# Clustered attention into an MLP on one core: a new order for the opening list, and a hand-over from attention to MLP in written order up to MLP step 14

## The chip, the cores and the metric

One core of a Trainium2 chip runs the whole program in one launch. The time is device microseconds of one execution; the figure given for a kernel is the median of several runs. The engines are TensorE (PE), VectorE (DVE), ScalarE (ACT), GpSimd (POOL) and SyncE (SP, which here only issues DMAs).

## The reference

Attention over 2 batches, 8 heads, 768 positions and 64 features, in which a query sees only the keys of its own cluster (argmax of the products with 16 normed centroids), followed by two MLP layers of 512 to 2048 to 512 on all 1536 tokens.

```python
q_assign = np.argmax(np.einsum('bhsd,hcd->bhsc', q_n, c_n), axis=-1)
k_assign = np.argmax(np.einsum('bhsd,hcd->bhsc', k_n, c_n), axis=-1)
mask = q_assign[:, :, :, None] == k_assign[:, :, None, :]
scores = np.where(mask, scale * np.matmul(q, k.transpose(0, 1, 3, 2)), -1000000000.0)
attn = np.exp(scores - np.max(scores, axis=-1, keepdims=True))
x = np.matmul(attn / (np.sum(attn, axis=-1, keepdims=True) + 1e-09), v)
...
h = x @ w_in
g = np.maximum(h, 0.0) + alpha * np.minimum(h, 0.0)
x = g @ w_out
...
h = x @ w_in2
return (np.maximum(h, 0.0) + np.log1p(np.exp(-np.abs(h)))) @ w_out2
```

## The kernel before

Matrix products run on PE in pairs of a high and a low part of each operand (a cast to fp32r, and what the cast left out), so that one product of the reference is two or three matmuls.

**Attention.** The work is cut into 8 pairs (batch, two heads) of 12 units each, so 96 units; a unit is 128 queries of one head against all 768 keys, and one unit is begun at every tick. A unit goes through `scores` (PE, L599 the products and L600 the cluster rows that serve as the mask), `maxima` (DVE, nm L605), `exps` (ACT, e L614), `transposes` (PE, pt L627), `highs` (ACT, ph L643), `lows` (DVE, pl L647), `attend` (PE, o L657) and `drain` (the copy tmp on ACT, L680 or L684, and the sum into xs on DVE or POOL, L682 or L691). While a pair is being worked on, the next pair's operands are made: `high_k`, `high_q` (ACT, hi L369, L372), `low_q` (DVE, lo L388), squares, folds and their norms (`inv_norm`, L131 to L140: ACT, then DVE or POOL), products with the centroids (dps L403), their copy (dsb L411), transposes (dt L428), normed products and one-hot rows (dn, mx, oh, L442 to L476), the mask rows (mq, mk, L507, L511). The tables STEADY, FIRST, SECOND, THIRD and LAST give for each of these steps the tick of the pair at which it is issued. The list PRELUDE is the order of the steps ahead of unit 0 and of those of pair 1 that stand with them ("hiq0 1" is `high_q` of the first half for pair 1; "warm 14" is 14 idle transposes on PE, wps L212). The order of instructions on the engines is the order in which the program issues them, by `man`, a manual schedule of all five engines, until `man.close()` at L814, which is tick 96 (NU): from there on a scheduler of the compiler orders the instructions.

**The end of a pair.** `finish` (L698) divides a pair's sums by its softmax sums and splits the result into xh and xl, the MLP's input: reciprocals (rs L721), their spread (rx, ACT L729), transposes (rp, PE L739), multiplication (xs, DVE L745), high (xh, ACT L752) and low part (xl, POOL L757). FINISH and FINISH_LAST give the ticks, counted from the pair's end.

**The MLP.** Two layers of 16 slices of 128 hidden features, in 3 groups of 512 tokens: 96 steps. Step k has a `first` product (hp, 12 matmuls, L876), an activation (`activate`: n and hp on ACT, L888, L889; `complete`: hp on DVE L909, gh on ACT L916, gl on DVE L917) and a `second` product (acc, 12 matmuls, L935); 96 x 24 = 2304 matmuls. BLOCKS groups the slices into runs whose sums stay in PSUM; `close` adds a run's sums to y (copy L947, additions L950). The weights come as float64 words and are converted on the chip: two halves of a slice (w_in, w_out), each one load and stages of m (ACT L164), r (ACT L167), L168, L171, L173 on DVE, t (POOL L178), high (ACT ih or oh, L180) and low (POOL il or ol, L181). There are five buffers for slices. Slices 0 and 1 are converted during the last attention ticks, their steps spread over the ticks; slices 2 to 6 in one go each, at these points:

```python
for F, k in ((2, -1), (3, 0), (4, 1)):
    due[k].append(F)
for F in range(5, 2 * NF):
    due.setdefault(last_use[F - 5], []).append(F)
```

The functions that the change touches stand here with the line numbers of the profile.

Of the kernel before, what the change touches and what calls it, by code (L numbers as in the profile page):

```python
# [9 lines left out]
F32 = mybir.dt.float32  # L10
# [23 lines left out]
    dl0=12, dl1=12, inv0=12, de0=12.5, de1=12.5, inv1=12.5, inv2=13, dt=13, dn=13.5, op0a=13.5, mx=14,  # L34
# [16 lines left out]
FINISH_LAST = [1, 2, 2, 3, 6, 7, 8, 9, 9]  # L51

BLOCKS = ((2, 4, 4, 4, 2), (4, 4, 4, 4))
P = 128
# [4 lines left out]
def kernel(  # L59
# [124 lines left out]
    def convert(F, pool, temp):  # L184
        layer, f = divmod(F, NF)
        w_in, w_out = (w_in1, w_out1) if layer == 0 else (w_in2, w_out2)
        tiles = [pool.tile([P, DM], F32R, tag=tag, name=tag) for tag in ("ih", "il", "oh", "ol")]
        weights[layer, f] = tiles
        return (
            to_float32(tiles[0], tiles[1], w_in[f].rearrange("p c n -> p (c n)"), temp),  # L190
            to_float32(tiles[2], tiles[3], w_out[f], temp),
        )


    with ExitStack() as actx:
# [110 lines left out]
        def steps_of(n):  # L306
# [56 lines left out]
            def high_k(t):  # L363
                if t == 0:
# [333 lines left out]
        def finish(n):  # L698
# [6 lines left out]
            ks = FINISH_LAST if last else FINISH  # L705
# [26 lines left out]

            for t in range(2):

                @at_(u0 + ks[4 + t])
                def _(t=t):
                    rp_ = ps_m.tile([P, 512], F32, tag="m", name="rp_")
# [6 lines left out]
                    xs = xs_[n]  # L744
                    nc.vector.tensor_tensor(out=xs[:, halves[t]], in0=xs[:, halves[t]], in1=rp_[:, 0:HS], op=ALU.mult)  # L745
# [36 lines left out]
        at(1)(lambda: warm(8))  # L782
# [29 lines left out]
        while u < NU + LAG + 2 or todo:  # L812
            if u == NU:
                man.close()  # L814
# [24 lines left out]
        man.close()  # L839

    gp = ctx.enter_context(tc.tile_pool(name="gp", bufs=2, reuse_waits="tile"))
    sp = ctx.enter_context(tc.tile_pool(name="sp", bufs=1, reuse_waits="tile"))
    cp = ctx.enter_context(tc.tile_pool(name="cp", bufs=2, side="right", reuse_waits="tile"))
    ps_h = ctx.enter_context(tc.tile_pool(name="ps_h", bufs=4, space=PSUM, reuse_waits="tile"))
    ps_a = ctx.enter_context(tc.tile_pool(name="ps_a", bufs=1, space=PSUM, reuse_waits="tile"))

    steps, starts, ends = [], set(), set()  # L850
    for layer in range(2):
        f0 = 0
        for size in BLOCKS[layer]:
            starts.add((layer, f0))
            ends.add((layer, f0 + size - 1))
            steps += [(layer, g, f) for g in range(NG) for f in range(f0, f0 + size)]
            f0 += size
    NS = len(steps)
    hps = {}
    mids = {}  # L860
    acts = {}
    accs = {}
    sums_ = {}

    def first(k):
        if k >= NS:
            return
        layer, g, f = steps[k]
        ts = slice(g * G, (g + 1) * G)
        h_, l_ = weights[layer, f][0:2]  # L870
        hp = ps_h.tile([P, G], F32, tag="h", name="hp")
        n = 0
        for c in range(NC_):
            cs = slice(c * P, (c + 1) * P)
            for a_, b_ in ((h_, xh), (h_, xl), (l_, xh)):
                nc.tensor.matmul(hp, lhsT=a_[:, cs], rhs=b_[:, c, ts], start=n == 0, stop=n == 3 * NC_ - 1)  # L876
                n += 1
        hps[k] = hp
# [194 lines left out]
```

## Time and profile before

| | |
|---|---|
| median of 3 runs | 807.25 us (805.39 to 807.45) |
| the profiled execution | 806.27 us |
| its span, first to last instruction | 804.5 us |
| mean granted TensorE clock | 0.987 |
| PE busy | 780.4 us, 97% |
| DVE busy | 585.3 us, 73% |
| ACT busy | 496.0 us, 62% |
| POOL busy | 356.8 us, 44% |

The span lies 1.8 us under the execution's own time. The profile's times are microseconds from the span's start. PE's matmuls overlap: a row's duration is longer than the distance to the next row, and it is the distance that counts. Of the span, attention takes roughly the first 270 us, the MLP the rest.

### The profile page before, as it was taken

What the parts mean: (1) busy time and instruction counts of PE and PEld (TensorE: products, weight loads), DVE (VectorE), ACT (ScalarE), POOL (GpSimd) and SP (SyncE); (2) the same over time, 40 slices, a digit from 0 to 9 for tenths busy, and PEclk for the clock granted to TensorE, in tenths of its full rate; (3) what the DMA queues carried; (4) which work ended last, traced back from release to release, by engine and by line L of the source; (5) the groups of instructions that cost most, each with busy time, mean ns of one, the idle gap of its engine ahead of it and who ended that gap; (6) DMA issues with size and microseconds to landing.
All of it is one profiled execution on the core that took longest, in us unless ns stands there. A gap on an engine that the chain in (4) does not pass through costs nothing.

```text
span 804.5 us, 11964 instructions
## 1 busy us (share of the span) xinstructions
PE 780.4 (97%) x4139; PEld 666.7 (83%) x4139; DVE 585.3 (73%) x923; ACT 496.0 (62%) x1024; POOL 356.8 (44%) x380
## 2 busy tenths in 40 slices
PE   6899999999998979999999999999999999999998
PEld 6789999999997758888888888888888888888886
DVE  7689989989989977547646835978469569765444
ACT  5788999999999778346536535674366245343221
POOL 6567668778354775026115404585144036023000
PEclk9899999999999989999999999999999999999999
DMA  9666667655552343102302401312014012000002
GB/s 265 180 166 172 152 170 173 182 145 128 119 144 64 105 157 132 53 26 79 105 0 72 138 1 53 132 53 78 1 53 156 2 53 81 24 2 1 28 31 97
DMA packets 26955, 75.91 MB, mean 94 GB/s; under 512 B 4464, under 2 KB 7408, under 8 KB 26896
## 3 DMA queue, kind: packets, MB, share of 16 engines
q1 hardware_dynamic: 26896, 75.16, 32.3%
q8 instruction: 32, 0.52, 0.3%
q14 instruction: 27, 0.22, 0.1%
HBM read 49.36 MB, written 3.15 MB: 65 GB/s over the span
## 4 chain that ended last, share of the span: by engine, by line
PE 78%; DVE 11%; ACT 3%; POOL 3%; issue 3%; DMA 1%; SPq 0%; DVEq 0%; POOLq 0%; ACTq 0%
PE acc L935 29%; PE hp L876 27%; PE pt L627 6%; PE o L657 6%; PE s L599 3%; PE s L600 3%; DVE r L173 2%; DVE pl L647 2%; POOL t L178 1%; DVE nm L605 1%; PE dps L403 1%; DVE m L168 1%; DVE y L950 1%; DVE lo L388 1%; ACT e L614 1%
## 5 line engine op out<-in xcount | busy, mean ns | idle before, releaser
L876 PE MATMUL hp<-xh,ih 128*128 128x512 f32 x384 | 150.2, 392 | 1.3 <-ACT e L614 1.3
L876 PE MATMUL hp<-xl,ih 128*128 128x512 f32 x384 | 150.1, 391 | 0.0
L876 PE MATMUL hp<-xh,il 128*128 128x512 f32 x384 | 149.9, 391 | 0.0
L181 POOL TENSOR_TENSOR il<-t,ih 128x512 fp32r<-128x512 f32 x32 | 44.3, 1385 | 198.7 <-ACT ih L180 188.3
L917 DVE TENSOR_TENSOR gl<-hp,gh 128x512 fp32r<-128x512 f32 x96 | 65.9, 686 | 69.6 <-ACT gh L916 69.5
L916 ACT CAST gh<-hp 128x512 fp32r<-128x512 f32 x96 | 56.4, 587 | 88.8 <-PE acc L935 69.9
L605 DVE TENSOR_REDUCE nm<-s 128x1 f32<-128x768 f32 x96 | 90.9, 947 | 18.3 <-PE s L600 18.3
L647 DVE TENSOR_TENSOR pl<-pt,ph 128x384 fp32r<-128x384 f32 x192 | 97.3, 548 | 5.8 <-ACT ph L643 4.9
L178 POOL TENSOR_TENSOR t<-m,r 128x512 uint32<-128x512 uint32 x64 | 85.6, 1337 | 30.8 <-DVE r L173 16.3
L643 ACT CAST ph<-pt 128x384 fp32r<-128x384 f32 x192 | 84.0, 485 | 14.7 <-PE pt L627 14.1
L614 ACT ACTIVATE e<-s,nm 128x768 f32<-128x768 f32 x96 | 87.9, 916 | 3.0 <-DVE nm L605 2.4
L898 ACT ACTIVATE sp<-a 128x512 f32<-128x512 f32 x48 | 30.4, 632 | 92.5 <-DVE a L894 92.5
L627 PE MATMUL pt<-ident,e 128*128 128x128 f32 x576 | 83.2, 277 | 4.1 <-DVE pl L647 4.0
L876 PEld LDWEIGHTS hp<-xh,ih 128*128 128x128 f32 x384 | 72.4, 189 | 16.5 <-ACT e L614 1.6
L876 PEld LDWEIGHTS hp<-xh,il 128*128 128x128 f32 x384 | 72.5, 189 | 15.2
L876 PEld LDWEIGHTS hp<-xl,ih 128*128 128x128 f32 x384 | 72.4, 189 | 15.1
L627 PEld LDWEIGHTS pt<-ident,e 128*128 128x128 f32 x576 | 66.9, 141 | 16.4 <-DVE pl L647 13.0
L935 PE MATMUL acc<-gh,oh 128*128 128x512 f32 x192 | 72.6, 395 | 5.4 <-ACT gh L916 5.4
L935 PE MATMUL acc<-gl,oh 128*128 128x512 f32 x192 | 75.7, 394 | 0.2 <-DVE gl L917 0.2
L935 PE MATMUL acc<-gh,ol 128*128 128x512 f32 x192 | 75.2, 392 | 0.0
L935 PE MATMUL acc<-ol,gh 128*128 128x512 f32 x192 | 74.7, 389 | 0.0
L935 PE MATMUL acc<-oh,gh 128*128 128x512 f32 x192 | 74.7, 389 | 0.0
(171 smaller groups left out, 1671.8 us busy)
## 6 DMA issues: line engine op xcount, KB each, us to landing
raw<-in_w_in_dram SPq DMA_DIRECT2D x32, 512.0 KB, 3.3
raw<-in_w_out_dram SPq DMA_DIRECT2D x32, 512.0 KB, 3.3
tok<-in_qk_tok_dram SPq DMA_DIRECT2D x8, 768.0 KB, 6.1
ak<-hi SPq DMA_DIRECT2D x31, 192.0 KB, 3.0
dim<-in_qk_dim_dram SPq DMA_DIRECT2D x6, 768.0 KB, 5.4
aq<-hi SPq DMA_DIRECT2D x16, 192.0 KB, 3.6
aq<-lo SPq DMA_DIRECT2D x16, 192.0 KB, 4.1
rawv<-in_v_dram SPq DMA_DIRECT2D x8, 384.0 KB, 3.5
```

What stands on the lines that cost most here:

```text
L178: nc.gpsimd.tensor_tensor(out=t.bitcast(U32), in0=mu, in1=r, op=ALU.add)
L181: nc.gpsimd.tensor_tensor(out=low, in0=t, in1=high.bitcast(F32), op=ALU.subtract)
L605: nc.vector.tensor_reduce(out=nm, in_=st[u]["s"][:, :, 0:HS], axis=AX.XY, op=ALU.max, negate=True)
L614: nc.scalar.activation(out=e.rearrange("p (a j) c -> p a (j c)", a=2), in_=st[u]["s"][:, :, 0:HS], func=AF.Exp, bias=st[u]["nm"], scale=1. ...
L627: nc.tensor.transpose(pt[:, j * P : (j + 1) * P], st[u]["e"][:, 3 * a + j, :], ident)
L643: nc.scalar.copy(out=dh, in_=src)
L647: nc.vector.tensor_tensor(out=dl, in0=src, in1=dh.bitcast(F32), op=ALU.subtract)
L657: nc.tensor.matmul(acc[key][:, 0:QG], lhsT=vv[:, j, 2 * hh : 2 * hh + 2, :].rearrange("p a d -> p (a d)"), rhs=grp[key][part][:, j, :], st ...
L876: nc.tensor.matmul(hp, lhsT=a_[:, cs], rhs=b_[:, c, ts], start=n == 0, stop=n == 3 * NC_ - 1)
L916: nc.scalar.copy(out=gh, in_=hp)
L917: nc.vector.tensor_tensor(out=gl, in0=hp, in1=gh.bitcast(F32), op=ALU.subtract)
L935: nc.tensor.matmul(accs[c], lhsT=a_, rhs=b_, start=opens and n == 0, stop=closes and n == 2)
```

## The change

It has two parts.

**The opening.** In PRELUDE the steps of pair 1 that cast its operands (hiq, hik), the centroid operands of pair 0 (op0a to op0c) and `values` stand ahead of pair 0's norm (inv0), and pair 1's low parts (lq0, lq1) stand around the norm and no longer behind the one-hot rows. Pair 2's inv2 comes half a tick later. The eight warm transposes at tick 1 are gone.

**The hand-over.** Pair 6 is finished at earlier ticks (FINISH_NEXT), pair 7 at nearer and in halves (FINISH_LAST; `multiply` and `rest_of_x` of their own). The conversions of slices 0 and 1 begin one tick earlier, the w_in halves first; slices 2 and 3 are no longer begun during the units. `head` puts slice 0's first product for token group 0 on PE at tick NU - 3 = 93, with its activation at 94 and 95, and that for group 1 (step 1 in the new blocks) at tick 99. The manual order goes on to MLP step 14; in it the tables BESIDE and LOADS say at which step a half of a slice is converted and loaded, and its last stage is issued a step later (`last_stages`). From step 14 on the scheduler orders as before. The first block of layer 0 has two slices and so has the second. The five weight buffers lie in two pools, of 2 and 3.

The diff, cut to what moves work:

```diff
 SECOND = dict(
-    dl0=12, dl1=12, inv0=12, de0=12.5, de1=12.5, inv1=12.5, inv2=13, dt=13, dn=13.5, op0a=13.5, mx=14,
+    dl0=12, dl1=12, inv0=12, de0=12.5, de1=12.5, inv1=12.5, dt=13, inv2=13.5, dn=13.5, op0a=13.5, mx=14,
...
 PRELUDE = [
...
-    "lq1 0", "sq0 0", "dk0 0", "dq0 0", "red0 0", "sq1 0", "dk1 0", "dq1 0", "red1 0", "inv0 0", "de0 0",
...
+    "lq1 0", "sq0 0", "dk0 0", "dq0 0", "red0 0", "sq1 0", "dk1 0", "dq1 0", "red1 0", "op0a 0", "op0b 0",
...
-FINISH_LAST = [1, 2, 2, 3, 6, 7, 8, 9, 9]
-
-BLOCKS = ((2, 4, 4, 4, 2), (4, 4, 4, 4))
+FINISH_LAST = [0.5, 1, 1, 1, 2, 4, 2, 4, 2]
+
+FINISH_NEXT = [3, 4, 5, 5, 6, 7, 7, 8, 9]
+
+BLOCKS = ((2, 2, 4, 4, 4), (4, 4, 4, 4))
+
+SLOTS = 5
+
+BESIDE = {2: (2, 1), 3: (3, 1), 4: (4, 0), 5: (4, 1), 6: (5, 0), 7: (6, 0), 8: (5, 1), 9: (6, 1), 12: (7, 0), 13: (7, 1)}
+
+LOADS = {3: 4, 5: 5, 6: 6, 11: 7}
...
-            ks = FINISH_LAST if last else FINISH
+            ks = FINISH_LAST if last else FINISH_NEXT if n == len(pairs) - 2 else FINISH
...
+            if last:
+                at_(u0 + ks[6])(lambda: rest_of_x(halves[0]))
+                at_(u0 + ks[7])(lambda: rest_of_x(halves[1]))
+            else:
+                at_(u0 + ks[8])(lambda: rest_of_x(slice(0, S)))
...
-        at(1)(lambda: warm(8))
...
-        for F in range(4):
-            todo[NU - 14 if F < 2 else NU - 12 + 6 * F, L].append(lambda F=F: begin(F))
-            for j in range(2):
-                start = NU - 12 + 3 * (2 * F + j)
-                for n, wait in enumerate((0, 2, 3, 4, 5, 6, 8) if F < 2 else (0,)):
-                    tick = NU - 14 if n == 0 and 2 * F + j < 3 else start + wait
-                    todo[tick, L].append(lambda F=F, j=j: next(started[F][j]))
+        for F in range(2):
+            todo[NU - 14, L].append(lambda F=F: begin(F))
+        for m, (j, F) in enumerate((j, F) for j in range(2) for F in range(2)):
+            for n, wait in enumerate((0, 2, 3, 4, 5, 6, 9)):
+                tick = NU - 14 if n == 0 and m < 3 else NU - 13 + 3 * m + wait
+                todo[tick, L].append(lambda F=F, j=j: next(started[F][j]))
+
+
+        def head(k):
+            if k == 0:
+                first(k, ps_m.tile([P, 512], F32, tag="m", name="hp"))
+            else:
+                both = ps_s.tile([P, 2, 512], F32, tag="s", name="hp")
+                first(k, both[:, 0])
+
+        todo[NU - 3, L].append(lambda: head(0))
+        todo[NU - 2, L].append(lambda: activate(0))
+        todo[NU - 1, L].append(lambda: complete(0))
+        todo[NU + 3, L].append(lambda: head(1))
+        todo[NU + 4, L].append(lambda: activate(1))
+        todo[NU + 5, L].append(lambda: complete(1))
...
-            if u == NU:
-                man.close()
...
-    for F, k in ((2, -1), (3, 0), (4, 1)):
-        due[k].append(F)
-    for F in range(5, 2 * NF):
-        due.setdefault(last_use[F - 5], []).append(F)
+    for F in range(8, 2 * NF):
+        due[max(14, last_use[F - SLOTS])].append(F)
...
+    def beside(F, j):
+        for _ in range(5):
+            next(fresh[F][j])
+        ready.append(fresh[F][j])
+
+    def last_stages():
+        while ready:
+            next(ready.pop())
...
+    for k in range(2, NS):
+        if k == 14:
+            man.close()
+        if k in LOADS:
+            load(LOADS[k])
...
         complete(k + 1)
-        if k < 2:
+        last_stages()
+        if k in BESIDE:
+            beside(*BESIDE[k])
+        if k >= 14:
             conversions(k)
         first(k + 2)
         activate(k + 2)
         second(k)
         close(k)
-        if k >= 2:
-            conversions(k)
```

How the instructions stand in a row, before and after, at three places (the changed kernel's line numbers differ from those of before). ACT in the opening, from pair 0's squares (sq) to pair 1's; before:

```order
L329 ACTIVATE sq<-tok 128x768 x2
L131 ACTIVATE s_236<-ss,tiny 128x24
L132 ACTIVATE s_236<-s_236 128x24
L411 COPY dsb<-dps 64x384 x2
L542 CAST mq<-hi 64x768
L369 CAST hi<-dim 128x384 x2
L372 ACTIVATE hi<-dim 128x384 x2
L329 ACTIVATE sq<-tok 128x768 x2
```

and now:

```order
L411 ACTIVATE sq<-tok 128x768 x2
L628 CAST mq<-hi 64x768
L458 ACTIVATE hi<-dim 128x384 x2
L454 CAST hi<-dim 128x384 x2
L138 ACTIVATE s_254<-ss,tiny 128x24
L139 ACTIVATE s_254<-s_254 128x24
L497 COPY dsb<-dps 64x384 x2
L411 ACTIVATE sq<-tok 128x768 x2
```

The mq copy and pair 1's casts (L369, L372; now L454, L458) have moved from behind the norm (s_236, s_254) and the copy of the centroid products (dsb) to ahead of both.

DVE in the opening, around pair 0's one-hot rows (oh), from the normed products to unit 0's maxima (nm); before:

```order
L442 TENSOR_TENSOR dn<-dt,rinv 128x384
L454 TENSOR_REDUCE mx<-dn 128x24
L462 TENSOR_TENSOR dn<-dn,mx 128x384
L463 TENSOR_TENSOR dn<-dn,rank 128x384
L473 TENSOR_REDUCE m_326<-dn 128x24
L476 TENSOR_TENSOR oh<-dn,m_326 128x384
L388 SCALAR_TENSOR_TENSOR lo<-dim,hi 128x384 x2
L511 TENSOR_SCALAR mk<-ot,mscale,mbias_96 16x384 x2
L605 TENSOR_REDUCE nm<-s 128x1 x2
```

and now:

```order
L474 SCALAR_TENSOR_TENSOR lo<-dim,hi 128x384
L528 TENSOR_TENSOR dn<-dt,rinv 128x384
L540 TENSOR_REDUCE mx<-dn 128x24
L548 TENSOR_TENSOR dn<-dn,mx 128x384
L549 TENSOR_TENSOR dn<-dn,rank 128x384
L559 TENSOR_REDUCE m_328<-dn 128x24
L562 TENSOR_TENSOR oh<-dn,m_328 128x384
L597 TENSOR_SCALAR mk<-ot,mscale,mbias_96 16x384 x2
L691 TENSOR_REDUCE nm<-s 128x1 x2
```

The two low parts of pair 1 no longer stand between the one-hot rows and the mask rows (mk); one of them stands ahead of the normed products, the other further up.

PE at the end of the units, from unit 95's scores (the last) to slice 0's first MLP product (hp); before:

```order
L599 MATMUL s<-ak,aq 128x384
L600 MATMUL s<-mk,mq 128x384
L627 MATMUL pt<-ident,e 128x128 x6
L657 MATMUL o<-pl,vv 128x256 x6
L739 MATMUL rp__4314<-ident,rx 128x128 x3
L627 MATMUL pt<-ident,e 128x128 x6
L876 MATMUL hp<-xh,ih 128x512
L876 MATMUL hp<-xl,ih 128x512
L876 MATMUL hp<-xh,il 128x512
```

and now, from the last units' transposes (pt) and attend matmuls (o) to the second product, that for token group 1:

```order
L743 MATMUL o<-ph,vv 128x256 x6
L713 MATMUL pt<-ident,e 128x128 x6
L743 MATMUL o<-pl,vv 128x256 x6
L743 MATMUL o<-ph,vv 128x256 x6
L831 MATMUL rp__4323<-ident,rx 128x128 x3
L743 MATMUL o<-pl,vv 128x256 x6
L831 MATMUL rp__4340<-ident,rx 128x128 x3
L232 MATMUL hp<-xh,ih 128x512
L232 MATMUL hp<-xl,ih 128x512
L232 MATMUL hp<-xh,il 128x512
```

The last attention work (o) and pair 7's reciprocals (rp) stand now ahead of that product; before, part of it stood behind the first hp product. The product for group 0 stands between the attend matmuls of one tick and the scores of unit 93:

```order
L713 MATMUL pt<-ident,e 128x128 x6
L743 MATMUL o<-pl,vv 128x256 x6
L232 MATMUL hp<-xh,ih 128x512
L232 MATMUL hp<-xl,ih 128x512
L232 MATMUL hp<-xh,il 128x512
```

## Rows read from the trace of the kernel before

**Rows 1.** The waits of PE: line waited for, us in total, times, longest.

```profile
PE acc L935 <- ACT gh L916: 5.4, 1, 5.4
```

**Rows 2.** Busy time by stretch (x instructions), then PE's granted clock, DMA share, GB/s.

```profile
22.00:32.00 10.00, 9.03 (x45) 7.68 (x43) 5.64 (x10) 5.91 (x16) 3.51 (x7) 0.67 0.74 215
...
80.00:240.00 160.00, 159.99 (x1201) 149.30 (x1200) 145.60 (x258) 149.82 (x365) 107.67 (x141) 1.00 0.61 153
...
250.00:260.00 10.00, 8.04 (x55) 6.69 (x56) 9.72 (x18) 9.06 (x22) 3.49 (x4) 1.00 0.35 114
```

**Rows 3.** Timeline of DVE, opening: start us, us, engine, line, operation.

```profile
14.49 0.57 DVE L463 TENSOR_TENSOR dn<-dn,rank 128x384 f32<-128x384 f32 x1
...
16.16 3.32 DVE L388 SCALAR_TENSOR_TENSOR lo<-dim,hi 128x384 fp32r<-128x384 f32 x2
...
19.51 1.26 DVE L511 TENSOR_SCALAR mk<-ot,mscale,mbias 16x384 fp32r<-16x384 f32 x2
```

**Rows 4.** Timeline of ACT, opening.

```profile
10.70 0.31 ACT L131 ACTIVATE s<-ss,tiny 128x24 f32<-128x24 f32 x1 [1.36 <-DVE ss L340]
...
11.90 0.84 ACT L542 CAST mq<-hi 64x768 fp32r<-64x768 f32 x1
...
13.46 0.94 ACT L372 ACTIVATE hi<-dim 128x384 fp32r<-128x384 f32 x2
```

**Rows 5.** Timeline of POOL, opening.

```profile
13.69 1.82 POOL L383 TENSOR_TENSOR lo<-dim,hi 128x768 fp32r<-128x768 f32 x1 [4.06 <-ACT hi L369]
...
15.95 5.09 POOL L348 TENSOR_TENSOR sq<-sq 128x768 f32<-128x768 f32 x6 [0.43 <-ACT sq L329]
```

**Rows 6.** Timeline of PE, opening.

```profile
16.70 0.53 PE L492 MATMUL ot<-identr,oh 128*64 128x128 f32 x6
...
20.92 0.41 PE L600 MATMUL s<-mk,mq 80*128 80x384 f32 x1 [3.47 <-DVE mk L511]
...
25.32 1.97 PE L212 MATMUL wps<-ident 128*128 128x128 f32 x8
```

**Rows 7.** Timeline of PE, hand-over and the program's last matmul.

```profile
263.92 0.61 PE L876 MATMUL hp<-xh,ih 128*128 128x512 f32 x1 [1.34 <-ACT e L614]
...
297.21 2.08 PE L935 MATMUL acc<-gh,oh 128*128 128x512 f32 x4 [5.38 <-ACT gh L916]
...
800.41 0.39 PE L935 MATMUL acc<-oh,gl 128*128 128x512 f32 x1
```

**Rows 8.** The chain that ended last, in order of time, about 305 us.

```profile
305.29 2.72 PE acc L935 x12
```

**Rows 9.** Timeline of DVE around the hand-over.

```profile
247.60 1.75 DVE L168 TENSOR_SCALAR m<-m 128x512 f32<-128x512 f32 x1
...
265.39 1.02 DVE L647 TENSOR_TENSOR pl<-pt,ph 128x384 fp32r<-128x384 f32 x2
...
266.42 1.49 DVE L173 SCALAR_TENSOR_TENSOR r<-raw,r 128x512 uint32<-128x512 uint32 x1
...
273.46 0.54 DVE L745 TENSOR_TENSOR xs<-xs,rp__4331 128x384 f32<-128x384 f32 x1
...
274.98 1.40 DVE L171 TENSOR_SCALAR m<-m 128x512 uint32<-128x512 uint32 x1
```

**Rows 10.** Timeline of ACT after the last unit's low parts.

```profile
269.98 0.36 ACT L680 COPY tmp<-o 64x256 f32<-64x256 f32 x1 [0.33 <-PE o L657]
```

**Rows 11.** Groups by line, all of the program: busy us, mean ns, idle before.

```profile
L173 DVE SCALAR_TENSOR_TENSOR r<-raw,r 128x512 uint32<-128x512 uint32 x64 | 61.8, 965 | 2.0 <-ACT r L167 1.0 <-issue 0.4
...
L950 DVE TENSOR_TENSOR y<-y,acc 128x512 f32<-128x512 f32 x84 | 54.9, 680 | 10.0 <-PE acc L935 10.0
...
L171 DVE TENSOR_SCALAR m<-m 128x512 uint32<-128x512 uint32 x64 | 48.8, 762 | 1.1
...
L168 DVE TENSOR_SCALAR m<-m 128x512 f32<-128x512 f32 x64 | 45.0, 704 | 12.4 <-ACT m L164 12.2
...
L909 DVE SCALAR_TENSOR_TENSOR hp<-n,nalpha,hp 128x512 f32<-128x512 f32 x48 | 35.9, 749 | 34.1 <-ACT hp L889 34.1
```

More of the change, by code (lines that the diff above doesn't have):

```diff
@@ L192, in convert, with first @@
         )
+    stage = {}
+    msteps, starts, ends = [], set(), set()
+    for layer in range(2):
+        f0 = 0
+        for size in BLOCKS[layer]:
+            starts.add((layer, f0))
+            ends.add((layer, f0 + size - 1))
+            msteps += [(layer, g, f) for g in range(NG) for f in range(f0, f0 + size)]
+            f0 += size
+    NS = len(msteps)
+    hps = {}
+    mids = {}
+    acts = {}
+    accs = {}
+    sums_ = {}
+    def first(k, hp=None):
+        if k >= NS:
+            return
+        layer, g, f = msteps[k]
+        ts = slice(g * G, (g + 1) * G)
+        h_, l_ = weights[layer, f][0:2]
+        if hp is None:
+            hp = stage["ps_h"].tile([P, G], F32, tag="h", name="hp")
+        n = 0
+        for c in range(NC_):
+            cs = slice(c * P, (c + 1) * P)
+            for a_, b_ in ((h_, xh), (h_, xl), (l_, xh)):
+                nc.tensor.matmul(hp, lhsT=a_[:, cs], rhs=b_[:, c, ts], start=n == 0, stop=n == 3 * NC_ - 1)
+                n += 1
+        hps[k] = hp
@@ L743, in _ @@
                         )
-                    xs = xs_[n]
-                    nc.vector.tensor_tensor(out=xs[:, halves[t]], in0=xs[:, halves[t]], in1=rp_[:, 0:HS], op=ALU.mult)
+                    if not last:
+                        multiply(t)
+                if last:
+                    at_(u0 + ks[4 + t])(lambda t=t: multiply(t))
             where = slice(b * S, (b + 1) * S)
@@ L848 @@
     ps_a = ctx.enter_context(tc.tile_pool(name="ps_a", bufs=1, space=PSUM, reuse_waits="tile"))
[L850 to L878, printed above, removed]
@@ L961, with slice_, load @@
     last_use = {}
-    for k, (layer, g, f) in enumerate(steps):
+    for k, (layer, g, f) in enumerate(msteps):
         last_use[layer * NF + f] = k
     due = defaultdict(list)
-    for F, k in ((2, -1), (3, 0), (4, 1)):
-        due[k].append(F)
-    for F in range(5, 2 * NF):
-        due.setdefault(last_use[F - 5], []).append(F)
+    for F in range(8, 2 * NF):
+        due[max(14, last_use[F - SLOTS])].append(F)
     def temp(which, dtype):
         return cp.tile([P, DM], dtype, tag=which, name=which, bufs=4 if which == "raw" else 2)
+    def slice_(F):
+        return convert(F, stage["wpool"] if F % SLOTS < 2 else wpool2, temp)
     def conversions(k):
         for F in due.get(k, []):
-            for gen in started.pop(F, None) or convert(F, stage["wpool"], temp):
+            for gen in slice_(F):
                 for _ in gen:
                     pass
-    conversions(-2)
-    first(0)
-    activate(0)
-    conversions(-1)
-    first(1)
-    complete(0)
-    activate(1)
-    for k in range(NS):
+    fresh = {}
+    ready = []
+    def load(F):
+        fresh[F] = slice_(F)
+        for gen in fresh[F]:
+            next(gen)
+    def beside(F, j):
[5 more added lines that the diff above has]
+            next(ready.pop())
+    load(2)
+    load(3)
+    second(0)
+    beside(2, 0)
+    first(2)
+    activate(2)
+    second(1)
+    close(1)
+    last_stages()
+    beside(3, 0)
+    first(3)
+    complete(2)
+    activate(3)
+    for k in range(2, NS):
[3 more added lines that the diff above has]
+            load(LOADS[k])
         if k == NS - 3:
```

108 lines of the change are left out of this document (58 added, 50 removed), and 9 rows, old and new, of the table PRELUDE.

## The prediction

> **What bounds the kernel now.** I read the windows first, then the waits of PE, then the timelines of two stretches: the opening (9 to 30 us) and the hand-over from the last attention units to the MLP (250 to 305 us). In the windows the reader sees that PE never stands from 80 to 240 us: 159.99 of 160 us busy at full clock [rows 2]. So time saved ahead of that stretch shifts all that follows, and time saved inside it on another engine is worth nothing. Two stretches differ: 22 to 32 us, where PE is busy 9.03 of 10 but at a granted clock of 0.67, and 250 to 260 us, where PE works 8.04 of 10 and DVE 9.72. The waits show one long stall behind that, 5.4 us on ACT's high part [rows 1], and the timelines show the rest: 3.47 us in the opening on DVE's mask rows [rows 6], 1.34 us ahead of the first MLP product [rows 7]. The program ends when PE does: its last matmul starts at 800.41 us [rows 7]; with the pitch of 2.72/12 = 0.23 [rows 8] PE ends at 800.64.
>
> **The opening.** (a) ACT: the copy to mq and four casts of pair 1 move ahead of the norm's first ACT step. They ran from 11.90 to 14.40, 2.50 us; ACT had stood 1.36 us before 10.70 [rows 4]. The norm starts 2.50 - 1.36 = 1.14 us later. (b) DVE: one low part of pair 1 now goes between rinv and dn. A two-input DVE operation of that shape took 0.57 [rows 3]; beside POOL the two low parts took 3.32, or 1.66 each [rows 3]. I take 0.57, since POOL has no fold to do that early; the other one goes into the time in which DVE now waits for the later norm. (c) The masks no longer stand behind these two. Their transposes were done at 16.70 + 0.53 = 17.23 [rows 6], the masks began at 19.51 [rows 3]: 2.28 us go. Unit 0's scores come 2.28 - 1.14 - 0.57 = 0.57 us earlier. (d) The eight warm matmuls ahead of unit 2's scores, 1.97 us of PE [rows 6], go; what lies next there are the products for unit 2, whose inputs were loaded early. Together 2.54; I take **2.5 us**. Bounds: with 1.66 in (b) and nothing from (d), because unit 2 then waits for its operands' DMAs, -0.5; with (b) hidden wholly, 3.1. The later first step of pair 2 (inv2 moved) costs nothing while POOL and DVE have gaps there; if they had none it would stay inside these bounds.
>
> A rule of the Trainium skill speaks against (b) and (c). The rows first: DVE's two-input subtraction at 14.49 took 0.57 while POOL's own subtraction ran from 13.69 to 15.51 [rows 3, 5], so it was not held up; the low parts, which began at 16.16 while POOL folded from 15.95 to 21.04, were [rows 3, 5]. SBUF — State Buffer, section "SBUF: two separate sides", in the Trainium skill says that DVE and GpSimd share a pair of ports by an exclusive lock, and that a DVE operation with two SBUF inputs blocks for the whole of the other's instruction. The first row disagrees, the second agrees. Without the rule the opening gives 2.5; with it, about nothing (rival C).
>
> **The hand-over.** Let T be the end of the last unit's low parts on DVE: before, 265.39 + 1.02 = 266.41 [rows 9]. From there to PE's end it took 800.64 - 266.41 = 534.23 us. What changes:
> (e) T moves back. Slice 0's first product (12 matmuls, 2.72 us by a chain row of 12 [rows 8]) now stands on PE ahead of unit 93's scores, and its activation puts two operations on DVE ahead of T: 0.75 for hp [rows 11] and about as much for the subtraction, 1.5. At most both count: 4.2. At least nothing: PE had 1.96 us free between 250 and 260 us [rows 2], and conversions that DVE does there could slide. DVE is at 9.72 of 10 [rows 2], so its 1.5 counts fully; the product comes ahead of PE's free time and delays the maxima on which DVE waits, so most of it counts. I take **3.6**, nearer the upper end: T = 270.0.
> (f) After T a short chain remains until slice 0's second product: the copy to tmp, the sum into xs, the transposed reciprocals, two multiplications. Before, tmp's start to the end of the multiplication was 269.98 to 274.00 [rows 9, 10], 4.0 us with other work between; without that work I take 3.7 (2.0 to 4.0).
> (g) From there PE has 2304 - 12 matmuls at 2.72/12 us [rows 8]: 519.5 us.
> (h) The clock: PE stands in (f), and after a stand it worked slowly. After 5.38 us, four matmuls took 2.08 us where 0.91 is their full-clock time; the first hp after 1.34 us took 0.61 [rows 7]. I take 2.0 in all: 1.2 from four, and a few more; ends 0 and 3.4 (twelve of them at that pace).
> (i) A new wait. Slice 7's first half is begun at step 12 and its last stage is at step 13, where product 15 reads it: no whole step of slack. DVE's part of a half conversion is 0.70 + 0.76 + 0.97 = 2.43 us at the means [rows 11], 1.75 + 1.40 + 1.49 = 4.64 when each is held up by POOL [rows 9]. A stall of 0 to 2.2; I take 1.0. The other conversions have a step or more. The late ACT high part that cost 5.38 us [rows 7] goes because slices 2 to 6 are now spread over steps instead of standing ahead of it in ACT's queue.
> Sum behind T: 3.7 + 519.5 + 2.0 + 1.0 = 526.2 against 534.23: 8.0 less, of which 3.6 is given back by T: **4.4 us** gained.
>
> In all 2.5 + 4.4 = 6.9 us off the profiled execution's 806.27 us, whose median of runs is 807.25 (0.98 more; I keep to the profiled one, which lies within the runs shown): 799.4, and I say **799.5**. A measurement of this kernel can tell 0.3%, 2.4 us, from no change: "same" is 804.8 to 809.7.
>
> **Rivals.**
> B, the units' end does not move and PE stays fast: the product fits into PE's free 1.96 us and DVE's slack, no low clock, no stall in (i). 799.5 - 3.6 - 2.0 - 1.0 = 792.9. For it: PE's free time before T; against: DVE at 9.72 of 10 [rows 2].
> C, the opening gives nothing: DVE's chain to the masks is held up by POOL's folds, which now begin earlier because the squares on ACT do. Two hold-ups of 1.3 to 1.8 us (a POOL operation is 1.82 [rows 5]) eat the 2.5. 802.0. For it the low parts' 1.66; against it the 0.57 [rows 3].
> D, no change: all at the far end, T back by 4.2, opening -0.5, (h) 2.6, (i) 2.2: 799.5 + 0.6 + 3.0 + 0.6 + 1.2 = 804.9.
> E, slower: the written order becomes the bound in steps 2 to 13. Engines do there what is written and can't fill a wait with later work. A step is 24 matmuls, 5.44 us. DVE needs 1.5 of it for the activation and, in three of these twelve steps, four additions of 0.68 [rows 11], 0.68 per step in the mean; that leaves 3.3 for a half conversion. At the held-up 4.64 [rows 9] each of twelve steps would be 1.3 longer: 16 us, 815. It decides from a mean of 4.15, where the loss of 0.85 x 12 = 10.2 lifts 799.5 over 809.7. Against it: the means sum to 2.43 over all 64 [rows 11].
> That the change doesn't do what it says I set aside: the order of instructions shows the moves.
>
> **How the numbers follow.** Forecast 0.50 (796.5 to 803 by its own bounds), B 0.14, C 0.17, D 0.11, E 0.08. The forecast, B and C are faster by over 0.3%, less 0.02 for their upper fringe: 0.79. Same: D and that fringe, 0.13. Slower: E, 0.08. The range runs from B's 793 to a little past D, 806; left out are E, half of B's lower side and D's upper side, under 0.2.
>
> **What would show it.** In the changed profile: no wait of PE on the mask rows near 3.5 us but one near 2.9, unit 2's scores about 2.5 us earlier; PE standing not over 1 us at a time from 245 us to T; T near 267.5, which is 270.0 less the opening's 2.5; slice 0's second product some 3.7 behind T at a low clock for a few matmuls; no 5.4 us on the high part; a wait of about 1 us at product 15. The forecast is wrong if T moves by more than 4.2 against the opening's shift (D), if PE waits in steps 2 to 13 again and again (E), or if unit 2's scores come no earlier (C).

## The result: slower, by the wait of one temporary, a late block and an opening that gives its gain back

| kernel | median us | runs | ratio to before, 95% interval |
|---|---|---|---|
| before, same chip | 806.28 | 805.39 to 807.45 | 1 |
| changed | 817.47 | 812.31 to 819.02 | 1.0117 (1.0098 to 1.0136) |
| changed, a second time beside another before (806.91) | 812.78 | 808.82 to 814.07 | 1.0070 (1.0047 to 1.0092) |

The forecast of 799.5 us, range 793 to 806, was wrong in its sign. The first measurement's three longer executions (817 to 819 us) have a mean granted TensorE clock of 0.981, the two shorter ones 0.986 and 0.987. The profiled execution of the changed kernel took 813.88 us, 7.6 more than before's 806.27, and its last matmul starts at 807.85 us for 800.41 [rows 7]. I use it for all that follows; PE's end is 0.23 later, as in the forecast.

The waits of PE in the changed kernel (line waited for, us in total, times, longest):

```profile
PE o L743 <- DVE xs L768: 6.3, 2, 4.5
PE dt L514 <- ACT dsb L497: 6.3, 2, 4.9
PE pt L713 <- DVE pl L733: 4.9, 6, 1.6
PE acc L973 <- DVE gl L273: 4.5, 3, 2.8
...
PE hp L232 <- ACT ih L187: 1.2, 1, 1.2
PE dps L489 <- DMA aq<-lo: 1.1, 1, 1.1
```

The 5.4 us on the high part gh [rows 1] are gone. What has come: 4.5 us of an attend matmul on xs, 4.9 in the opening (on the same copy of the centroid products, dsb, before waited 2.1 at the longest), 2.8 of a second product on the low part, and the 1.2 of product 15 that the forecast had named. The windows show the stretch of the units' end in the changed kernel (columns as in [rows 2]: PE, PEld, DVE, ACT, POOL, granted clock):

```profile
250.00:260.00 10.00, 9.56 (x67) 8.21 (x67) 8.99 (x15) 7.18 (x18) 5.08 (x5) 1.00 0.22 67
260.00:270.00 10.00, 7.39 (x45) 5.61 (x43) 6.96 (x13) 7.86 (x18) 4.16 (x4) 1.00 0.00 1
270.00:280.00 10.00, 5.01 (x24) 4.71 (x25) 4.74 (x11) 5.49 (x12) 1.22 (x3) 0.66 0.00 0
```

and, behind the 8.04 us of PE from 250 to 260 us [rows 2], in before:

```profile
260.00:270.00 10.00, 8.38 (x44) 6.98 (x44) 9.87 (x16) 8.66 (x20) 7.85 (x6) 0.83 0.23 81
270.00:280.00 10.00, 10.00 (x57) 8.60 (x56) 8.81 (x14) 7.18 (x14) 5.75 (x5) 1.00 0.39 131
```

In the changed kernel no engine is full from 260 to 280 us: all wait for one another. The granted clock averages 0.66 from 270 us on, part of the stretch at each of its two levels (0.5 is 1.2 GHz, 1 is 2.4 GHz). The cause stands in ACT's and POOL's timelines. ACT:

```profile
256.28 0.64 ACT L187 CAST ih<-t 128x512 fp32r<-128x512 f32 x1
259.74 0.66 ACT L174 ACTIVATE r<-raw 128x512 uint32<-128x512 uint32 x1 [2.82 <-POOL t L185]
260.31 0.89 ACT L700 ACTIVATE e<-s,nm 128x768 f32<-128x768 f32 x1
...
267.25 0.67 ACT L187 CAST ih<-t 128x512 fp32r<-128x512 f32 x1
270.78 0.66 ACT L174 ACTIVATE r<-raw 128x512 uint32<-128x512 uint32 x1 [2.86 <-POOL t L185]
271.34 0.57 ACT L272 CAST gh<-hp 128x512 fp32r<-128x512 f32 x1
271.93 0.36 ACT L766 COPY tmp<-o 64x256 f32<-64x256 f32 x1
272.32 0.90 ACT L700 ACTIVATE e<-s,nm 128x768 f32<-128x768 f32 x1
```

and POOL:

```profile
257.00 1.28 POOL L188 TENSOR_TENSOR il<-t,ih 128x512 fp32r<-128x512 f32 x1 [4.49 <-ACT ih L187]
258.23 1.47 POOL L185 TENSOR_TENSOR t<-m,r 128x512 uint32<-128x512 uint32 x1
...
268.06 1.47 POOL L188 TENSOR_TENSOR il<-t,ih 128x512 fp32r<-128x512 f32 x1 [5.84 <-ACT ih L187]
269.49 1.26 POOL L185 TENSOR_TENSOR t<-m,r 128x512 uint32<-128x512 uint32 x1
```

The temporary r of a conversion has one buffer. The change issues a half conversion's last stage (ih, il) one tick later against its other stages, wait 9 for 8. In that tick POOL now has il of one half ahead of t of the next, and ACT has r of the half after that directly behind ih. So ACT's r waits for t, t stands behind il, and il waits for ih on ACT: 0.6 + 1.3 + 1.5 us in a row, twice, while behind ACT's r the exps of the last units and the copy to tmp wait. PE's timeline shows what follows from it, and the waits behind (in the first row the attend matmul that wants xs, which wants tmp; the third row is slice 0's first product for token group 1, the fourth product 15, and the last one stands at the end of layer 0):

```profile
273.14 1.65 PE L743 MATMUL o<-ph,vv 128*128 128x256 f32 x6 [4.47 <-DVE xs L768]
...
279.20 0.98 PE L743 MATMUL o<-ph,vv 128*128 128x256 f32 x6 [1.85 <-DVE xs L768]
...
281.46 0.48 PE L232 MATMUL hp<-xh,ih 128*128 128x512 f32 x1
...
356.95 0.50 PE L232 MATMUL hp<-xh,ih 128*128 128x512 f32 x1 [1.19 <-ACT ih L187]
...
376.02 0.50 PE L973 MATMUL acc<-gl,oh 128*128 128x512 f32 x1 [1.55 <-DVE gl L273]
...
562.46 0.96 PE L973 MATMUL acc<-oh,gl 128*128 128x512 f32 x3 [2.77 <-DVE gl L273]
```

The difference in three pieces, cut at unit 80's scores and at the end of the last unit's low parts, which in the changed kernel are this row of DVE:

```profile
275.98 1.20 DVE L733 TENSOR_TENSOR pl<-pt,ph 128x384 fp32r<-128x384 f32 x2 [0.91 <-ACT ph L729]
```

Unit 80's scores start at 224.57 us (before 221.43): 3.1 us lost in the opening and the units behind it. From there to the end of unit 95's low parts it took 52.6 us; the forecast had 270.0 - 221.43 = 48.6. From these low parts to PE's end it took 530.9 us; the forecast had 526.2. So against the forecast 5.6 us are missing in the opening (it had 2.5 gained), 4.0 at the units' end and 4.7 behind, 14.4 in all (rounded). Against before, cut at the same two places, the last two pieces took 52.6 us for 51.5 and 530.9 for 527.7: the change lost 3.1, 1.1 and 3.2 us there.

### The profile page after: what moved, and what is told of

The parts are those of the page before. It is cut to its first block, busy times and chain, and to the rows that moved or that the text cites. A ratio compares the mean times of both kernels' runs of the same rounds, so it can differ in the third digit from the quotient of the medians.

```text
span 811.9 us, 11952 instructions
## 1 busy us (share of the span) xinstructions
PE 779.9 (96%) x4131; PEld 666.3 (82%) x4131; DVE 580.5 (71%) x923; ACT 495.6 (61%) x1024; POOL 355.2 (44%) x381
## 4 chain that ended last, share of the span: by engine, by line
PE 81%; DVE 6%; ACT 4%; POOL 4%; issue 3%; DMA 1%; SPq 0%; POOLq 0%; DVEq 0%; ACTq 0%
PE acc L973 30%; PE hp L232 28%; PE o L743 7%; PE pt L713 7%; PE s L685 4%; PE s L686 3%; DVE r L180 2%; DMA tok<-in_qk_tok_dram 1%; PE dps L489 1%; POOL sq L430 1%; DVE m L175 1%; ACT e L700 1%; ACT ph L729 1%; POOL t L185 1%; DVE y L988 1%
## 5 line engine op out<-in xcount | busy, mean ns | idle before, releaser
L713 PE MATMUL pt<-ident,e 128*128 128x128 f32 x576 | 85.0, 281 | 5.0 <-DVE pl L733 4.9
L973 PE MATMUL acc<-oh,gl 128*128 128x512 f32 x192 | 73.7, 390 | 2.8 <-DVE gl L273 2.8
```

Source lines behind the costliest of these rows:

```text
L713: nc.tensor.transpose(pt[:, j * P : (j + 1) * P], st[u]["e"][:, 3 * a + j, :], ident)
L973: nc.tensor.matmul(accs[c], lhsT=a_, rhs=b_, start=opens and n == 0, stop=closes and n == 2)
```

## Experiments

Ratios are to before on the same chip, with 95% intervals; about 0.3% (2.4 us) can be told apart. Where two changed kernels are compared, their ratios often come from two chips.

**The two parts alone.** The opening alone is before with the new PRELUDE and SECOND and without `warm(8)`; the hand-over alone is the changed kernel with before's:

```diff
-    "lq1 0", "sq0 0", "dk0 0", "dq0 0", "red0 0", "sq1 0", "dk1 0", "dq1 0", "red1 0", "op0a 0", "op0b 0",
+    "lq1 0", "sq0 0", "dk0 0", "dq0 0", "red0 0", "sq1 0", "dk1 0", "dq1 0", "red1 0", "inv0 0", "de0 0",
...
+        at(1)(lambda: warm(8))
```

> The opening's part of the change alone, the hand-over as before. Theory: the moved casts wait on ACT for the load of dim for pair 1 and hold up pair 0's norm behind them, and the later operands of pairs 1 and 2 lead to short stands of PE after which its clock falls; by the changed kernel's trace unit 16's scores come 3.1 us later than before. Expected here: 3 to 6 us slower than before, scores of unit 0 1 us or more later, PE's dt behind a wait of over 4 us. Rival: the late load was a matter of that one execution; then within 2 us of before, and unit 4's scores earlier by 1 to 3 us. Second rival, my forecast's: 2.5 us faster.

Measured: 1.0010 (0.9993 to 1.0026), eleven executions from 803.8 to 811.9 us. The profiled one took 2729 us for a reason that is not known; the ratio is without it, and its trace is not read. The opening alone is worth nothing in the mean; the 3 to 6 us of my theory were those of one execution.

> The hand-over's part of the change alone, the opening as before. Theory: two waits of ACT of 2.9 us each, for r behind POOL's t, delay the units' end by more than the forecast 3.6; by the trace 7.7 lost up to the end of the low parts of unit 95 and 3.3 won back behind it. Expected here: 4 to 5 us slower than before. Rival: the loss is the opening's and grows into the hand-over; then within 2 us of before or faster.

Measured: 1.0089 (1.0076 to 1.0102), 7.2 us slower. The loss is the hand-over's. Both waits of ACT on t are in its trace, 5.7 us together, while the scores of units 2 to 88 start within 0.1 us of before's.

**The wait for r, from three sides.** First the tick of the last stage undone, then a second buffer for r with the order of all instructions kept, and later (below) three repairs without that buffer:

```diff
-            for n, wait in enumerate((0, 2, 3, 4, 5, 6, 9)):
+            for n, wait in enumerate((0, 2, 3, 4, 5, 6, 8)):
```

> The changed kernel with the last stage of the four half conversions one tick earlier again (wait 8 for 9), so that POOL's il and ol no longer come in the same tick ahead of the next half's t. Theory: ACT's two waits of 2.8 and 2.9 us for r behind t go or fall under 1 us; PE's 4.5 us on xs goes; 4 to 7 us faster than the changed kernel. Rival: the units' end is late because of the early product on PE and its activation on DVE and ACT; then ACT waits elsewhere and the time is within 1.5 us of the changed kernel.

Measured: 1.0092 (1.0079 to 1.0106). ACT's waits on t fell to one of 0.9 us and PE's 4.5 on xs to 2.3, as expected, and the stretch from unit 80's scores to the last low parts from 52.6 to 50.2 us. The time did not follow: from the low parts to PE's end it took 534.3 for 530.9 us. So the wait is named rightly, but undoing the tick doesn't win its price. Where it was given back, the trace shows in part: behind the low parts PE's waits are 0.5 us longer in all, and the granted clock is 0.76 from 274 to 281 us and 0.57 from 560 to 564, where the changed kernel's was 1.00 from 278 us on.

```diff
-            return stage["cpool"].tile([P, DM], dtype, tag=which, name=which, bufs={"raw": 3, "m": 2, "t": 2}.get(which, 1))
+            return stage["cpool"].tile([P, DM], dtype, tag=which, name=which, bufs={"raw": 3, "m": 2, "t": 2, "r": 2}.get(which, 1))
```

> The changed kernel with a second buffer for r in the conversions of slices 0 and 1, the order of all instructions as in the changed kernel. Theory: the wait of ACT's r was on its single buffer, which POOL's t of the half before still reads; with two buffers both waits of 2.8 and 2.9 us go and the time is 4 to 7 us under the changed kernel's, like with the earlier last stage. Rival: the wait moves one instruction on (ACT's next step waits for t, or DVE's do), and under 1.5 us is won.

Measured: 1.0034 (1.0015 to 1.0052), which is 0.4 to 0.8% under the changed kernel's two ratios. ACT no longer waits for t in this stretch, and unit 80 to the last low parts takes 49.6 us, 3.0 less, with nothing moved. The waits of ACT between 240 and 285 us in this kernel:

```profile
ACT xh L847 <- DVE xs L821: 4.6, 2, 3.5
ACT ph L729 <- PE pt L713: 3.6, 3, 2.0
ACT n L244 <- PE hp L232: 3.5, 2, 1.8
ACT gh L272 <- DVE hp L265: 0.9, 2, 0.6
ACT rx L815 <- DVE rs L807: 0.8, 1, 0.8
```

In this one execution, though, the 3.0 us were not kept: from the low parts to PE's end it took 534.9 us for 530.9, with waits no longer than the changed kernel's but more of the stretch at the lower clock:

```profile
260.00:270.00 10.00, 6.13 (x32) 5.24 (x30) 7.00 (x15) 7.00 (x16) 3.16 (x4) 0.68 0.00 0
270.00:280.00 10.00, 8.52 (x35) 7.66 (x36) 2.15 (x5) 3.60 (x9) 4.46 (x4) 0.64 0.32 102
```

So the buffer's price rests on the medians here, and on the pair of kernels at the end of this section.

**The block at the layer's end** (on the kernel with two r buffers, as the next ones):

```diff
-BLOCKS = ((2, 2, 4, 4, 4), (4, 4, 4, 4))
+BLOCKS = ((2, 2, 4, 4, 2, 2), (4, 4, 4, 4))
```

> The kernel with two r buffers, and layer 0's blocks as (2, 2, 4, 4, 2, 2) for (2, 2, 4, 4, 4): the layer ends on two slices again, as before the change. Theory: the wait of 2.8 us at the layer's boundary comes from the last block of four, whose slots come free late, so that conversions, the closing additions and the next layer's high and low parts fall together on DVE; it falls under 0.5 us and 2 to 3 us are won on the kernel with two r buffers. Rival: DVE is as full with more closings (12 more additions of 0.68 us), the wait stays or moves, and under 1 us is won.

Measured: 0.9998 (0.9985 to 1.0011), 2.9 us better than with two r buffers by the ratios, and its trace has no wait of PE at the layer's boundary. DVE's timeline in the changed kernel shows what filled that place: conversions for layer 1, ahead of the low part that PE waits for. They take 1.51, 1.18 and 1.49 us beside POOL, which is busy up to 562.93; the same three lines behind that take 0.41, 0.68 and 0.43:

```profile
557.18 1.51 DVE L175 TENSOR_SCALAR m<-m 128x512 f32<-128x512 f32 x1
558.61 0.68 DVE L250 TENSOR_SCALAR a<-hp 128x512 uint32<-128x512 uint32 x1
559.21 1.18 DVE L180 SCALAR_TENSOR_TENSOR r<-raw,r 128x512 uint32<-128x512 uint32 x1
560.31 1.49 DVE L178 TENSOR_SCALAR m<-m 128x512 uint32<-128x512 uint32 x1
561.73 0.68 DVE L273 TENSOR_TENSOR gl<-hp,gh 128x512 fp32r<-128x512 f32 x1
```

**The early product.**

```diff
-        todo[NU - 3, L].append(lambda: head(0))
-        todo[NU - 2, L].append(lambda: activate(0))
-        todo[NU - 1, L].append(lambda: complete(0))
+        todo[NU - 1, L].append(lambda: head(0))
+        todo[NU, L].append(lambda: activate(0))
+        todo[NU + 1, L].append(lambda: complete(0))
```

> The kernel with two r buffers, and slice 0's first product at tick 95, behind the last unit's scores, for tick 93, its activation two ticks later too. Theory: of the 4.5 us by which the units' end is still late, 2.7 are the product ahead of unit 93's scores and up to 2 are the activation ahead of unit 95's exps; the end of the last low parts comes 3 to 4.5 us earlier, and since the product fills PE's stands at the units' end, 2.5 to 4.5 us are won in all. Rival: the units' end is set by DVE and ACT work that stays (pair 6's finish, conversions); under 1 us is won.

Measured: 1.0033 (1.0020 to 1.0047), as without it. The last low parts come 0.6 us earlier and PE waits 3.7 us for xs behind them in one piece. The rival holds: the product that I had priced as the main cause of a later end costs nearly nothing there.

> Before's opening with the changed hand-over, two r buffers, the product at tick 95 and blocks (2, 2, 4, 4, 2, 2). Theory: hand-over 7.1 us slower than before as it stands in the change; less 3 to 4 for the buffer, 2.5 to 4.5 for the product and 2 to 3 for the blocks: 0.5 to 5 us faster than before, about 803.5. Rival: the three gains overlap (the same wait is taken away twice), and it is within 2 us of before.

Measured: 0.9995 (0.9986 to 1.0004): within 2 us of before, so one of the three, the product, gave nothing.

**Slice 7.**

```diff
-BESIDE = {2: (2, 1), 3: (3, 1), 4: (4, 0), 5: (4, 1), 6: (5, 0), 7: (6, 0), 8: (5, 1), 9: (6, 1), 12: (7, 0), 13: (7, 1)}
+BESIDE = {2: (2, 1), 3: (3, 1), 4: (4, 0), 5: (4, 1), 6: (5, 0), 7: (6, 0), 8: (5, 1), 9: (6, 1), 11: (7, 0), 12: (7, 1)}
```

> The kernel with two r buffers, and slice 7's halves converted one step earlier, at steps 11 and 12. Theory: the wait of 1.2 us of product 15 on slice 7's high part goes, since it has a step more; 1 to 1.5 us are won. Rival: its load is issued at step 11 too, so that ACT waits about 3 us for it with step 13's activation queued behind, and nothing is won or up to 2 us are lost.

Measured: 0.9996 (0.9982 to 1.0010). The 1.19 us are gone, and with them the 1.55 us of the second product near 371 us. The ratio moved by 3.1 us for 2.7 us of waits.

**The repairs together.** The three edits shown above, two r buffers, blocks that end on two slices and slice 7 a step earlier, in the changed kernel, and then in the one with before's opening:

> The changed kernel with two r buffers, blocks (2, 2, 4, 4, 2, 2) and slice 7 one step earlier, all three. Theory: the three waits are separate, so their prices add: 1.2 and 2.7 us less than with two r buffers alone, 4 us together, 2 to 4 us faster than before, near 804. Rival: a wait that goes lets another grow, and it is no faster than the better of the two alone, within 1 us of before.

Measured: 0.9936 (0.9919 to 0.9954), 802.05 us for 807.20: faster than both kernels. The prices add within the noise: 7.9 us less than with two r buffers alone, for 2.9 and 3.1. PE's stands of over 0.15 us from 240 us on sum to 6.3 us here, 14.0 in the changed kernel and 9.2 in before. PE's waits that are left behind unit 80 are 1.25 us on pl, 2.25 and 1.85 on xs, and four under 0.5; the first two groups of its waits, the opening's included:

```profile
PE o L743 <- DVE xs L768: 4.1, 2, 2.2
PE pt L713 <- DVE pl L733: 4.0, 5, 1.6
```

> The same three repairs with before's opening. Theory: the new opening is worth nothing in the mean of many executions, only its spread is wider; then this is within 1.5 us of the kernel with the new opening, and its executions lie closer together. Rival: the new opening's gain of 1 to 2 us at unit 4 lasts in most executions; then this one is 1.5 us or more slower.

Measured: 0.9948 (0.9930 to 0.9966). The new opening makes no difference that can be told.

**The opening's pieces,** on the kernel before: only `warm(8)` taken out, and only the new order with `warm(8)` kept.

```diff
-        at(1)(lambda: warm(8))
```

> Before with the eight warm matmuls at tick 1 taken out and nothing else. Theory: they cost PE 2 us ahead of unit 2's scores, so those come up to 2 us earlier, and since PE then waits for pair 2's low parts or operands, less than 1 us of it is left at unit 20. Rival: all of it is kept, 1.5 to 2.5 us faster; second rival: without them the clock falls in the units behind, 1 to 3 us slower.

Measured: 0.9999 (0.9984 to 1.0013). Unit 4's scores came 1.7 us earlier than in before's profiled execution, unit 20's 0.6; both lie within what four traces with before's opening show (table below).

> Before with the new order of the opening list and the later first step of pair 2's norm, and the eight warm matmuls kept. Theory: ACT's casts wait for the load of pair 1's operands with the norm behind them, so unit 0's scores come 0.5 to 2 us later than before; at unit 4 the difference is 0 to 2 us, and the time within 2 us of before. Rival, my forecast's (a) to (c): unit 0's scores 0.6 us earlier and the time 0.5 to 1 us faster.

Measured: 0.9988 (0.9975 to 1.0000); unit 4's scores 1.9 earlier, unit 20's 1.1. The first mask product, for which PE had waited 3.47 us [rows 6], started at 20.23 for 20.92, 0.7 earlier, where (a), (b) and (c) together forecast 0.57.

**The sum once more:** the changed kernel again, the three repairs less the buffer, and the three with the last stage at wait 8.

> The changed kernel as it is, once more, beside the two that follow on the same chip. Theory: 1.0 to 1.5% slower than before, and the slower of its executions (817 to 819 us) have a lower mean granted clock than the faster ones (812 to 814 us). Rival: the first five executions were an unlucky chip; then it is 0.6 to 0.9% slower like its hand-over alone.

Measured: 1.0070 (1.0047 to 1.0092); the second measurement lies under the first, whether by the chip or by the executions is not shown, and the change costs 0.7 to 1.2%. All waits from 240 us on are those of the first trace to 0.05 us, and unit 80 to the last low parts takes 52.6 us again.

> The kernel with all three repairs less the second r buffer: blocks (2, 2, 4, 4, 2, 2) and slice 7 one step earlier alone. Theory: ACT's two waits of 2.9 us come back and with them PE's 4.5 us on xs and a low clock behind it; 3 to 7 us slower than with all three. Rival: with the other waits gone the units' end matters less, and under 2 us come back.

Measured: 0.9991 (0.9977 to 1.0005), 4.4 us slower than with all three, and from unit 80's scores to PE's end 5.1 us more in the traces (579.0 for 573.9). The buffer's price stands from both sides. ACT's first wait between 240 and 285 us is back:

```profile
ACT r L174 <- POOL t L185: 5.7, 2, 2.9
```

> All three repairs, and the last stages one tick earlier as well (wait 8 for 9). Theory: with two r buffers ACT no longer waits for t, so the tick of the last stage is worth nothing more: within 1 us of the three repairs. Rival: ACT's ih ahead of POOL's il a tick earlier takes POOL's time from the next t, and it is 1 to 3 us slower or faster.

Measured: 0.9975 (0.9962 to 0.9988), 3.1 us slower than without it: unit 80 to the last low parts takes 50.9 us for 49.4. With two buffers the later last stage is the better one, which agrees with the little that the earlier one won alone; which work the earlier stage delays was not followed.

## Why the prediction was wrong

**(a) to (c), the first scores: right in the sum when the loads come as before, in part by luck.** In the eight traces with the new order in which tok had landed by 7.8 us, the norm started at 11.3 to 11.7, 0.6 to 1.0 behind before's 10.70 [rows 4]; the forecast said 1.14. The first mask product started at 20.1 to 20.5 for 20.92, a gain of 0.4 to 0.8; the forecast said 0.57. (In the five traces with before's order it started at 20.3 to 20.9, so the gain in the mean is nearer 0.4.) Two terms were off and cancelled. A hold-up of 0.96 us was not in the sum: a two-input step of the norm on DVE took 1.13 to 1.15 us in all eleven traces with the new order and 0.18 to 0.19 in the five with before's, because POOL's subtraction for pair 1, which the earlier casts brought forward, now stands beside it (rows under (d)). Against it, the norm came less late than I said, and in the trace of the new order alone the low part added 0.2 to the chain where I had 0.57. What I left out besides is that these steps stand behind loads. In the profiled execution of the change tok landed 1.35 us later, and dim for pair 1 after it; ACT's casts waited, and the norm behind them:

```profile
9.10 1.58 ACT L411 ACTIVATE sq<-tok 128x768 f32<-128x768 f32 x2 [2.28 <-DMA tok<-in_qk_tok_dram]
...
11.74 0.94 ACT L458 ACTIVATE hi<-dim 128x384 fp32r<-128x384 f32 x2 [0.34 <-DMA dim<-in_qk_dim_dram]
...
13.40 0.31 ACT L138 ACTIVATE s<-ss,tiny 128x24 f32<-128x24 f32 x1
```

**(d), and "time saved ahead of 80 us shifts all that follows": wrong.** That sentence was the step that failed in the opening. The scores of units 4 and 20 in the traces of all kernels with one opening or the other:

| opening | traces | unit 4, mean us | unit 20, mean us | unit 20, range |
|---|---|---|---|---|
| before's | 4 | 30.45 | 74.58 | 74.07 to 74.97 |
| the change's | 10 | 29.37 | 75.52 | 73.36 to 78.02 |

The gain is there at unit 4, 1.1 us in the mean, and at unit 20 it is a loss of 0.9 us in the mean. Between them stand the products with the centroids for pair 2, whose operands hang on loads and on POOL, not on PE. PE came earlier and waited there. In the changed kernel's trace, POOL (first two rows) and PE:

```profile
33.16 1.47 POOL L413 TENSOR_TENSOR sq<-tok 128x768 f32<-128x768 f32 x1 [1.75 <-DMA tok<-in_qk_tok_dram]
34.59 2.15 POOL L469 TENSOR_TENSOR lo<-dim,hi 128x768 fp32r<-128x768 f32 x1
```

```profile
36.79 0.39 PE L489 MATMUL dps<-lo,chz 128*64 128x384 f32 x1 [0.77 <-POOL lo L469]
38.63 0.39 PE L489 MATMUL dps<-lo,chz 128*64 128x384 f32 x1 [1.10 <-DMA aq<-lo]
```

and the windows there:

```profile
36.00:40.00 4.00, 2.13 (x9) 1.60 (x9) 2.58 (x3) 1.77 (x5) 2.16 (x2) 0.88 0.97 213
40.00:44.00 4.00, 4.00 (x23) 3.79 (x22) 2.53 (x4) 1.85 (x4) 0.70 (x1) 0.69 0.98 265
```

PE worked 2.13 of the first 4 us, and in the next 4 at a granted clock of 0.69, so that the wait was paid twice. In the trace with two r buffers the same opening had PE at 3.27 us of the same window and the clock stayed at 1.00:

```profile
36.00:40.00 4.00, 3.27 (x22) 3.07 (x23) 2.69 (x6) 2.83 (x7) 0.00 (x0) 1.00 0.82 168
40.00:44.00 4.00, 3.95 (x30) 3.50 (x29) 3.50 (x6) 2.77 (x8) 3.51 (x3) 1.00 1.02 272
```

There the gain of 1.6 us at unit 20 was kept. In six of ten traces with the new opening, units 4 to 8 took over 15 us, in the other four and in the four with the old one 12.8 to 14.0. The clock divides them: from 36 to 44 us its mean is 0.79 in each of these six and 1.00 in all the other eight. PE waits there with either opening, 1.93 us in one piece in a trace of the old one whose clock stayed at 1.00. Why the clock fell in these six stays open. Rival C had the right result for the opening alone; of its mechanism there was one hold-up in DVE's chain to the one-hot rows, by POOL's subtraction and not by its folds:

```profile
14.34 1.14 DVE L143 TENSOR_TENSOR s<-ss,s 128x24 f32<-128x24 f32 x1
...
17.75 0.57 DVE L548 TENSOR_TENSOR dn<-dn,mx 128x384 f32<-128x384 f32 x1
```

The second row is an operation with two inputs that took 0.57 us beside POOL's folds (17.47 to 22.17 us). The first took 1.14 for the 0.18 us of its like; it ended as POOL's subtraction of 13.63 us did, at 15.4. The rule of the Trainium skill, SBUF — State Buffer, section "SBUF: two separate sides", that a DVE operation with two SBUF inputs blocks while GpSimd's instruction holds the shared ports, agrees with the first. On the second it is silent: the kernel keeps pair 0's dn in PSUM (`ps_s`), so only one input comes from SBUF. The same holds for the row at 14.49 us [rows 3], which I had read as speaking against the rule; neither row speaks against it.

**(e), the units' end: wrong twice.** First, I had the wrong row. The low parts at 265.39 us [rows 9] are unit 94's; unit 95's stand in the same trace of before, behind slice 0's first product:

```profile
271.93 1.02 DVE L647 TENSOR_TENSOR pl<-pt,ph 128x384 fp32r<-128x384 f32 x2
```

So the units ended at 272.95 us, and PE had some twenty matmuls of the MLP behind it by then; the 534.23 us with which I compared were no measure of the old hand-over: from the right row it is 800.64 - 272.95 = 527.7 us, so that the forecast's 526.2 behind T saved 1.5 us and not 8.0. The forecast of the changed kernel, though, was an absolute one (T = 270.0 from unit 80's 221.43, 48.6 us; so it lay 2.9 us ahead of before's 272.95, where I meant 3.6 behind), and that came out 4.0 short. Second, the price: I gave the product on PE and its activation 3.6 us. Moving the product away won nothing, and the wait of r for POOL's t, which I had not in the sum, cost 3.0 in this stretch (52.6 to 49.6 with two buffers; 53.1 to 49.4 in the repaired kernel). I counted for the moved last stage what it costs each engine, not what stands in POOL's queue between it and the next user of a single buffer. The remaining 1 us is the difference between the 49.6 measured and the 48.6 forecast; its cause stays open.

**(f) to (i), behind the units.** The tail (f) took 281.46 - 277.18 = 4.3 us for 3.7. The clock's cost (h), 2.0 in the forecast, was nothing behind it:

```profile
280.00:800.00 520.00, 514.26 (x2271) 424.61 (x2270) 340.52 (x498) 256.20 (x457) 182.67 (x137) 1.00 0.19 65
```

The low clock lay mostly ahead of T (0.51 in the mean from 271 to 278 us), where three groups of six matmuls took 1.65, 1.48 and 1.63 us for the 0.98, 1.01 and 0.95 of their like. What is left of 808.08 - 281.46 = 526.6 us after 519.5 of matmuls and 5.7 of waits, 1.4 us, lies nearly all in the matmuls next to the stands, which are further apart than pitch and idle time account for. The wait (i) on slice 7 was 1.19 for 1.0. But the sum of waits was 5.7: 0.23, 1.19, 1.55 and 2.77. The 2.77 is the layer's boundary, 280 us behind the hand-over, where I had not looked: BLOCKS was changed for the hand-over and moved the last block from two slices to four.

**The rivals.** E, the written order as the bound in steps 2 to 13, didn't happen: PE waited there 0.23 and 1.19 us. The slower case came from places that no rival named: POOL's queue at the units' end, and the block at the layer's end. D, all at the far end, was nearest with 804.9 (it took 2.6 for (h), whose end I had put at 3.4); it lacks these 3.0 and 2.8 us and most of what the opening lost. One sign against the forecast could be read at once: PE was not to stand over 1 us at a time up to T, and it stood 4.47.

## What to carry to other kernels

Where a hand-written order moves a stage by a tick, follow every single-buffered temporary round its loop of engines (here ACT ih, POOL il, POOL t, ACT r): a queue that is empty by the profile of before can close such a loop, and a second buffer was worth 0.4 to 0.8% here. Time won ahead of a stretch in which PE is full shifts it only if the loads and the other engines' work for the next stage come earlier too and PE's clock holds; ask at each later point what PE will wait for. A constant that is changed for one place (the block sizes) has to be followed to every place that reads it.

## What was not expected of the hardware

A stand of PE is paid again in clock, and not always. After waits of 0.77 and 1.10 us (2.13 of 4 us busy) the granted clock was 0.69 in the next 4 us. Further on the same transposes waited 1.58 us in the changed kernel's trace (at 61.97 us) and 1.57 in before's (at 60.29), with PE busy 2.42 and 2.43 of the 4 us from 58 to 62; from 62 to 66 us the granted clock was 0.62 in the changed kernel and 1.00 in before. So the length of the wait and the work around it did not tell the two apart. The same kernel spreads over 10 us in the first and second measurement (808.8 to 819.0), where before spreads over 5 (804.6 to 809.8); I put this down to the clock and the landing of the loads, and no run separates the two.
